# An attention block with two feed-forward layers: sums of the first block products drawn ahead, and the last stores of the first layer moved to ScalarE's queue

## The chip, the cores and the metric

The kernel runs on one core of a Trainium2 chip, in one launch. The metric is the device time in microseconds (us). Five engines have instruction streams of their own: TensorE (PE; its weight loads are shown as PEld), VectorE (DVE), ScalarE (ACT), GpSimd (POOL) and SyncE (SP). SP does no arithmetic here; it issues DMA transfers, one after the other in its program's order, and a transfer whose condition is not met holds up all that stand behind it. ScalarE can issue transfers as well, in the order of its own stream. An instruction on any engine starts when the semaphores that it waits for have been raised by the instructions or transfers that it depends on.

## The reference, cut to what matters

```python
# q, k, v: 4 batches x 8 heads x 768 positions x 64;  mem_k, mem_v: 8 positions more
for c in range(768 // 32):                  # chunks of 32 queries
    k_ctx, v_ctx = positions 32c-16 .. 32c+40, cut at the ends
    scores = (q_c @ concat(mem_k, k_ctx).T) / 8
    a = exp(scores - max); a = a / (sum(a) + 1e-9)
    out_c = a @ concat(mem_v, v_ctx)
x = out as 3072 tokens x 512
h = x @ w_in                                # 512 x 2048
x = maximum(0.01 * h, h) @ w_out            # 2048 x 512
out = ((x @ w_a) * (x @ w_b)) @ w2_out      # 512 x 1536, 512 x 1536, 1536 x 512
```

All values are float32.

## The kernel before, in words

**Precision.** TensorE is fed with a rounded part and a remainder of each operand: ScalarE casts a tile to the rounded type ("hi", names like `xh`, `gh`, `ch`), VectorE subtracts it from the original ("lo", `xl`, `gl`, `cl`), and each product is three matmuls: hi·hi, hi·lo, lo·hi.

**Blocks and items.** The 3072 tokens are six blocks of 512, counted from 0. For blocks 0 to 3 the first layer runs as a list of items (block, f), where f is one of 16 slices of 128 hidden units. An item has 12 matmuls `h<-xh,w`, `h<-xl,w` (lines 435 to 437), a leaky relu on ScalarE (`g<-h`, L527), its cast (`gh<-g`, L530) and remainder (`gl<-g,gh`, L533), and two items later 12 matmuls of `mm2` (L559 to 563) that add to four PSUM banks `a`. At the last f of a block, `mm2` copies each of the four banks with ScalarE to a tile `x2` (written `x` in the trace, tag `z`, three buffers), and SP stores it to the block's DRAM array `x2d` (L576, L577). In this text item i means the i-th of the items of blocks 0 to 3 (i = 16 · block + f), so the last is item 63.

**Attention beside the items.** The 24 attention units (128 tokens each) run between the items. `STARTS` says at which item unit k of the last sixteen begins: scores and the first half of the softmax at item i, the rest of the softmax at i+1, sixteen 32-wide transposes on VectorE (`pt<-p`, L348) at i+2, and at i+3 the product with the values on TensorE (`pv<-pt,v`, L388) and a copy of it into the token tiles (`a_out`; `a_raw` for blocks 4 and 5, into `xr`). A unit of block 4 that is done before `xr` exists (item 48) is stored to DRAM (`x4d`) and read back. The preparation of the second layer's weights is spread over the same items.

**Block products.** Blocks 4 and 5 of the first layer go together through seven products of half-size blocks instead of eight. Token sums `y` come from `xr` (VectorE subtractions in `y_sub`, ScalarE cast and VectorE remainder in `y_part`), weight sums from `w` (`s_sums`: two additions `zs`, tag `z`, and four `sc`; `s_parts`: cast and remainder `sw`). `prod` runs six matmuls into a bank `A`, `B` or `C`; a loop over p takes the 16 slices in eight pairs. In it, `snapped` copies a bank to a tile `u` with ScalarE, `summed` adds a bank to it on VectorE (`s`), and the sum goes through the leaky relu (`g<-s`) and `mm2`. TensorE, VectorE and ScalarE keep the written order here (class `InOrder`; its helper lines L46 and L49 stand for the line in many rows). SP's order comes from a scheduler.

**What comes behind.** Block 5 ends with 16 calls of `mm2` on kept values, with w_out tiles read back on SP (`wo_load`, L853). Its last call again makes four copies and four stores. The second layer follows: `wab_load` (L1094) fetches weights (`wab<-wab`, 512 KB each, five buffers in a pool that takes the place of the first layer's weight pool), and its first matmuls are `ca<-ch,wab`, six to a bank. `xs_load` (L803) reads blocks of `x2d` back for it.

Of the kernel before, what the change touches and what calls it, by code (L numbers as in the profile page):

```python
# [55 lines left out]
def kernel(  # L56
# [355 lines left out]
    def x_raw():  # L412
        for h, tag in enumerate(("xh", "xl")):
            xr[NL + h] = xp.tile([P, KC, TB], F32, tag=tag, name="xr")
        for k in x4d:
            sp.dma_start(out=xr[NL][:, :, k * UT:k * UT + UT], in_=x4d[k])
# [10 lines left out]
    def x_tiles(key):  # L427
        hi = xp.tile([P, KC, TB], F32R, tag="xh", name="xh")
        lo = xp.tile([P, KC, TB], F32R, tag="xl", name="xl")
        x1[key] = (hi, lo)  # L430
# [109 lines left out]
    def mm1(bi, parts):  # L540
        return mm1_act(*mm1_pe(bi, parts))

    def mm2(bi, parts, g):
        if bi not in acc:
            last = bi == NB3 - 1
            acc[bi] = [
                p.tile([P, TB], F32, tag=t, name="a")
                for p, t in (((ps_h, "h"), (ps_s, "s")) * 2 if last else ((ps_a, "a"),) * KC)
            ]
        gh, gl = g  # L550
        for o, n, f in parts:
            slot = wslot[f, 1]
            t = slice(o, o + n)
            for e in range(KC):
                ps = acc[bi][e][:, t]
                c = slice(e * P, e * P + P)

                kw = dict(skip_group_check=bi == 0)
                pe.matmul(  # L559
                    ps, slot[:, 1, c], gh[:, t], start=f == 0 and o == 0, stop=False, **kw  # L560
                )
                pe.matmul(ps, slot[:, 0, c], gl[:, t], start=False, stop=False, **kw)  # L562
                pe.matmul(  # L563
                    ps, slot[:, 0, c], gh[:, t], start=False,
                    stop=f == NF1 - 1 or (o == HALF and f == LEAD - 1), **kw
                )
            if bi == 0:
                ready = {(0, NF1 - 1): slice(0, HALF), (HALF, LEAD - 1): slice(HALF, TB)}
                t = ready.get((o, f))
            else:  # L570
                t = t if f == NF1 - 1 else None
            if t is not None:
                for e in range(KC):
                    ps = acc[bi][e][:, t]
                    y = tp.tile([P, TB], F32, tag="z", name="x2", bufs=3)
                    act.copy(y[:, t], ps)  # L576
                    sp.dma_start(out=x2d[bi][:, e, t], in_=y[:, t])  # L577

    HALF, LEAD = TB // 2, 3
    items = []  # L580
# [94 lines left out]
    def at_item(i, *args):  # L675
        at(*divmod(i, NF1), *args)

    STARTS = (17, 20, 23, 26, 29, 32, 34, 37, 40, 42, 45, 48, 50, 53, 56, 59)
    for k, i in enumerate(STARTS):
        u = 2 * TB // UT + k  # L680
        blk, o = divmod(SEQ[u], TB // UT)
# [19 lines left out]
    def prep_load(upto):  # L701
        while len(raws) < min(upto, len(sources)):
            raw = prep.tile([P, 512, 2], I32, tag="raw", name="raw", bufs=4)
            nc.sync.dma_start(
                out=raw.rearrange("p n w -> p (n w)"),
                in_=w2_l[sources[len(raws)]].bitcast(I32),
            )
            raws.append(raw)
# [138 lines left out]
    def wo_load(upto):  # L847
        while wo_next[0] < upto:
            b, f = 1 + wo_next[0] // NF1, wo_next[0] % NF1
            if b == NB3:  # L850
                break
            t = wop.tile([P, 2, 512], F32R, tag="wo", name="w")
            nc.sync.dma_start(out=t.bitcast(F32), in_=wod[f])  # L853
            wslot[f, 1] = t
            wo_next[0] += 1

    x_tiles(("x", 1))
    behind += first_items()
    STEPS = 58
    for bi, f, parts in items[LEAD:]:  # L860
        first = bi == 0
        if f == 0 and not first:
            if bi + 1 < NL:
                x_tiles(("x", bi + 1))
            else:
                x_raw()
        if first:
            W1.load(2 * f + 14)
            W1.step()
        behind.append((bi, parts, mm1(bi, parts)))  # L870
        if first:
            W1.step()
        if len(behind) > LAG:
            mm2(*behind.pop(0))
        for fn in beside.get((bi, f), []):
            fn()
        if not first:
            wo_load((bi - 1) * NF1 + f + 4)

            i = (bi - 1) * NF1 + f  # L880
            n = (NL - 1) * NF1
            for _ in range(STEPS * (i + 1) // n - STEPS * i // n):
                next(steps, None)
        elif f >= NF1 - 1:
            wo_load(f - NF1 + 2)
            prep_load(f - NF1 + 1)


    att.__exit__(None, None, None)
    xa_pool = tc.tile_pool(name="xa", bufs=1, side="left", reuse_waits="tile")  # L890
    xa = xa_pool.__enter__()
    ya, hc, homes = {}, KC // 2, {}
    two = "p k n -> p (k n)"

# [11 lines left out]
        return homes[key][:, h]  # L906

    def y_part(i):
        t = Y[i].rearrange(two)
        hi, lo = [y_home(i, l) for l in range(2)]  # L910
        ya[i] = hi, lo
        hi, lo = hi.rearrange(two), lo.rearrange(two)
        act.copy(hi, t)
        dve.tensor_tensor(out=lo, in0=t, in1=hi.bitcast(F32), op=ALU.subtract)

    b11, b21, b12, b22 = [
        xr[NL + h][:, k * hc:k * hc + hc] for h in range(2) for k in range(2)
    ]
    Y = (b11, b21, b21, b12, b12, b11, b22)

    def y_sub(out, x, y):
        dve.tensor_tensor(out=out, in0=x, in1=y, op=ALU.subtract)

    sums_, sw = {}, {}

# [18 lines left out]
    def s_parts(p, h):  # L944
        t = sums_[p][h]
        w = xa.tile([P, 2, 2, 256], F32R, tag="sw", name="sw", bufs=3)
        act.copy(w[:, 0], t)
        dve.tensor_tensor(out=w[:, 1], in0=t, in1=w[:, 0].bitcast(F32), op=ALU.subtract)
        for k, n in enumerate(((2, 3), (4, 6))[h]):
            sw[p, n] = w[:, :, k]  # L950

    def prod(ps, p, n, i, first):
# [6 lines left out]
        for kc in range(hc):  # L959
# [3 lines left out]
            pe.matmul(ps, w[:, 0, c], lo[:, kc], start=False, stop=False, **kw)  # L963
            pe.matmul(ps, w[:, 0, c], hi[:, kc], start=False, stop=kc == hc - 1, **kw)

    def relu(src, kept=None):
        g = tp.tile([P, TB], F32, tag="t", name="g")
        act.activation(g, src, AF.Prelu, alpha=0.01)
        if kept is None:
            gh = tp.tile([P, TB], F32R, tag="gh", name="gh", bufs=3)  # L970
            gl = tp.tile([P, TB], F32R, tag="gl", name="gl", bufs=3)
        else:
            w = wp.tile([P, 2, TB], F32R, tag=f"wi{kept}", name="g5")
            gh, gl = w[:, 0], w[:, 1]
        act.copy(gh, g)

        def low():
            dve.tensor_tensor(out=gl, in0=g, in1=gh.bitcast(F32), op=ALU.subtract)
            return gh, gl

        return low

    def snapped(ps):
        t = tp.tile([P, TB], F32, tag="t", name="u")
        act.copy(t, ps)
        return t
# [17 lines left out]
    def part2(bi, f, g):  # L1004
        return bi, [(0, TB, f)], g

    y_part(0)
    y_part(1)
    next2(behind.pop(0))
    y_sub(b12, b12, b11)  # L1010
    y_part(3)
    y_sub(b12, b22, b12)
    s_sums(0)
    s_parts(0, 0)
    y_part(4)
    y_sub(b11, b12, b11)
    y_part(5)
    s_parts(0, 1)
    y_sub(b21, b21, b12)
    y_part(2)  # L1020
    y_part(6)

    kept, late = {}, None
    for p in range(NF1 // 2):
        f0, f1 = 2 * p, 2 * p + 1
        A = ps_h.tile([P, TB], F32, tag="h", name="A")
        prod(A, p, 0, 0, True)
        Bk = ps_s.tile([P, TB], F32, tag="s", name="B")
        if p:
            act.copy(Bk, A)  # L1030
            low12 = relu(late, f1 - 2)
        else:
            a1 = snapped(A)
        next2(behind.pop(0))
        if p:
            kept[f0 - 2] = low12()
        prod(Bk, p, 1, 1, p == 0)
        if p:
            next(steps, None)
        if p + 1 < NF1 // 2:  # L1040
            s_sums(p + 1)
        low11 = relu(Bk if p else summed(a1, Bk))
        g11 = low11()
        prod(A, p, 2, 4, False)
        u2 = snapped(A)
        C = ps_s.tile([P, TB], F32, tag="s", name="C")
        prod(C, p, 3, 3, True)
        if p + 1 < NF1 // 2:
            s_parts(p + 1, 0)
            s_parts(p + 1, 1)  # L1050
        prod(A, p, 4, 5, False)
        u3 = snapped(A)
        s22 = summed(u3, C)
        next2(part2(NL, f0, g11))
        kept[f1] = relu(s22, f0)()
        if p:
            next(steps, None)
        prod(A, p, 5, 2, False)
        low21 = relu(A)
        prod(C, p, 6, 6, False)  # L1060
        behind.append(part2(NL, f1, low21()))
        late = summed(u2, C)
# [519 lines left out]
```

## Time and profile before

| | |
|---|---|
| time, median of 3 runs | 1146.26 us (1146.11 to 1147.21) |
| the profiled execution's own time | 1146.38 us |
| its span in the profile | 1144.6 us |
| TensorE busy | 1105.0 us (97%) |
| VectorE busy | 776.0 us (68%) |
| ScalarE busy | 527.3 us (46%) |
| mean granted TensorE clock | 0.987 |
| DMA moved | 270.63 MB, mean 236 GB/s |

The profile is of one execution. A row of the timeline gives the start, the duration, the engine, the line, the operation with out<-in and, in square brackets, how long the engine was idle before it and what ended that idle time. A row "x3" sums up three instructions in a run. In window rows "PEclk" is the mean granted TensorE clock as a share of full speed: 1.00 is 2.4 GHz, 0.50 is 1.2 GHz. The time of the profiled execution is 1.78 us longer than its span.

### The profile page before, as it was taken

What the parts mean: (1) busy time and instruction counts of PE and PEld (TensorE: products, weight loads), DVE (VectorE), ACT (ScalarE), POOL (GpSimd) and SP (SyncE); (2) the same over time, 40 slices, a digit from 0 to 9 for tenths busy, and PEclk for the clock granted to TensorE, in tenths of its full rate; (3) what the DMA queues carried; (4) which work ended last, traced back from release to release, by engine and by line L of the source; (5) the groups of instructions that cost most, each with busy time, mean ns of one, the idle gap of its engine ahead of it and who ended that gap; (6) DMA issues with size and microseconds to landing.
All of it is one profiled execution on the core that took longest, in us unless ns stands there. A gap on an engine that the chain in (4) does not pass through costs nothing.

```text
span 1144.6 us, 16319 instructions
## 1 busy us (share of the span) xinstructions
PE 1105.0 (97%) x6194; PEld 912.8 (80%) x6194; DVE 776.0 (68%) x1418; ACT 527.3 (46%) x893; POOL 6.3 (1%) x16
## 2 busy tenths in 40 slices
PE   7899999999999995999997999999999999999997
PEld 6788888888888883888886888888888888888886
DVE  6897389888988765666540555668755668755666
ACT  5886555556555434565521343233343233343232
POOL 2000000000000000000000000000000000000000
PEclk9999999999999997999998999999999999999999
DMA  9996799999999912443485947476877476757452
GB/s 322 396 354 234 247 350 328 338 314 337 322 321 338 332 70 92 157 157 133 164 338 173 309 135 252 134 251 188 242 240 251 136 249 188 235 176 248 139 194 74
DMA packets 99854, 270.63 MB, mean 236 GB/s; under 512 B 9664, under 2 KB 24128, under 8 KB 99008
## 3 DMA queue, kind: packets, MB, share of 16 engines
q1 hardware_dynamic: 98608, 268.93, 69.7%
q8 instruction: 49, 0.80, 0.3%
q10 hardware_dynamic: 1168, 0.66, 0.2%
q14 instruction: 29, 0.24, 0.1%
HBM read 215.02 MB, written 54.53 MB: 235 GB/s over the span
## 4 chain that ended last, share of the span: by engine, by line
PE 92%; DVE 2%; ACT 2%; DMA 2%; issue 1%; SPq 0%; DVEq 0%; ACTq 0%
PE ca L49 18%; PE cc L49 9%; PE oa L49 8%; PE a L49 8%; PE h L435 5%; PE a L559 5%; PE h L436 5%; PE h L437 5%; PE a L562 5%; PE a L563 5%; PE cb L49 5%; PE oy L49 4%; PE A L49 4%; PE pv L388 2%; PE s L279 2%; PE C L49 2%
## 5 line engine op out<-in xcount | busy, mean ns | idle before, releaser
L49 PE MATMUL ca<-ch,wab 128*128 128x512 f32 x576 | 193.1, 391 | 6.3 <-DMA wab<-wab 6.3
L49 ACT CAST st<-gb 128x512 fp32r<-128x512 f32 x126 | 76.5, 621 | 124.4 <-DVE gb L49 121.0
L49 PEld LDWEIGHTS ca<-ch,wab 128*128 128x128 f32 x576 | 108.6, 189 | 29.7 <-issue 6.7
L49 PE MATMUL ca<-cl,wab 128*128 128x512 f32 x288 | 112.6, 391 | 0.0
L49 PE MATMUL oa<-st,wt 128*128 128x512 f32 x420 | 104.3, 389 | 0.0
L435 PE MATMUL h<-xh,w 128*128 128x512 f32 (+1 forms) x256 | 101.7, 397 | 0.7 <-ACT xh L49 0.7
L49 PE MATMUL cc<-ch,wab 128*128 128x512 f32 x288 | 100.3, 389 | 0.0
L436 PE MATMUL h<-xl,w 128*128 128x512 f32 (+1 forms) x256 | 98.7, 386 | 0.2 <-DVE xl L49 0.2
L437 PE MATMUL h<-xh,w 128*128 128x512 f32 (+1 forms) x256 | 98.7, 385 | 0.0
L559 PE MATMUL a<-gh,w 128*128 128x512 f32 (+1 forms) x256 | 97.7, 382 | 0.3 <-ACT x L576 0.3
L562 PE MATMUL a<-gl,w 128*128 128x512 f32 (+1 forms) x256 | 97.5, 381 | 0.0
L563 PE MATMUL a<-gh,w 128*128 128x512 f32 (+1 forms) x256 | 97.4, 381 | 0.0
L49 DVE TENSOR_TENSOR st<-gb,st 128x512 fp32r<-128x512 f32 x126 | 85.3, 689 | 15.0 <-ACT st L49 13.2
L49 PEld LDWEIGHTS oa<-st,wt 128*128 128x128 f32 x420 | 78.8, 188 | 16.4
L49 ACT COPY u<-ca 128x512 f32<-128x512 f32 x72 | 42.3, 587 | 92.4 <-PE ca L49 92.3
L348 DVE STREAM_TRANSPOSE pt<-p 32x128 f32<-32x128 f32 x256 | 77.4, 302 | 4.3
L49 PEld LDWEIGHTS ca<-cl,wab 128*128 128x128 f32 x288 | 54.3, 189 | 11.1
L49 PEld LDWEIGHTS cc<-ch,wab 128*128 128x128 f32 x288 | 54.1, 188 | 11.3
L533 DVE TENSOR_TENSOR gl<-g,gh 128x512 fp32r<-128x512 f32 (+1 forms) x64 | 43.2, 675 | 22.2 <-ACT gh L530 18.5
L435 PEld LDWEIGHTS h<-xh,w 128*128 128x128 f32 x256 | 48.1, 188 | 11.3 <-ACT xh L49 0.8
L559 PEld LDWEIGHTS a<-gh,w 128*128 128x128 f32 x256 | 48.1, 188 | 10.1 <-ACT x L576 0.8
L49 PE MATMUL cc<-cl,wab 128*128 128x512 f32 x144 | 56.0, 389 | 0.0
(189 smaller groups left out, 2043.3 us busy)
## 6 DMA issues: line engine op xcount, KB each, us to landing
wab<-wab SPq DMA_DIRECT2D x126, 512.0 KB, 4.4
w<-wod SPq DMA_DIRECT2D x80, 512.0 KB, 5.4
raw<-w SPq DMA_DIRECT2D x68, 512.0 KB, 6.9
wt<-wtd SPq DMA_DIRECT2D x63, 512.0 KB, 4.7
k<-kl SPq DMA_DIRECT2D x48, 256.0 KB, 5.3
v<-vl SPq DMA_DIRECT2D x48, 256.0 KB, 5.1
wab<-pwb SPq DMA_DIRECT2D x12, 768.0 KB, 6.9
wod<-w SPq DMA_DIRECT2D x16, 512.0 KB, 6.6
```

What stands on the lines that cost most here:

```text
L49: self.last = emit(*args, **kwargs).ins
L279: pe.matmul(s[64 * cpar:64 * cpar + 64, cp * 4 + hp, :], qb[:, o, :], k[:, r:r + 64], start=True, stop=True,)
L348: dve.transpose(out=pt[o0:o0 + 32, :, 2 * cpar + hpar, hpx, :], in_=p[i0:i0 + 32, hpx::2, 32 * b:32 * b + 32],)
L388: pe.matmul(o[64 * hpar:64 * hpar + 64, 2 * pair:2 * pair + 2, t0:t0 + CH], v[:, i:i + 64], pt[:, 2 * cp + pair, 2 * cpar + hpar].rearrang ...
L435: pe.matmul(ps, w[1], x[0], start=first, stop=False)
L436: pe.matmul(ps, w[0], x[1], start=False, stop=False)
L437: pe.matmul(ps, w[0], x[0], start=False, stop=last)
L533: dve.tensor_tensor(out=gl[:, c], in0=g[:, c], in1=gh[:, c].bitcast(F32), op=ALU.subtract)
L559: pe.matmul(ps, slot[:, 1, c], gh[:, t], start=f == 0 and o == 0, stop=False, **kw)
L562: pe.matmul(ps, slot[:, 0, c], gl[:, t], start=False, stop=False, **kw)
L563: pe.matmul(ps, slot[:, 0, c], gh[:, t], start=False, stop=f == NF1 - 1 or (o == HALF and f == LEAD - 1), **kw)
```

## The change

Three things change, and no matmul is added or taken away. The last block's four stores are issued by ScalarE instead of SP. The last eight attention units begin zero, one or two items earlier: 40, 42, 45, 48, 50, 53, 56, 59 become 39, 42, 44, 47, 49, 52, 54, 57. And part of the token and weight sums of the first block products is attached to items 60, 61 and 62 instead of standing behind item 63; what is left is spread over the first pass of the loop over p.

```diff
-                    sp.dma_start(out=x2d[bi][:, e, t], in_=y[:, t])
+                    (act if bi == NB3 - 1 else sp).dma_start(out=x2d[bi][:, e, t], in_=y[:, t])
...
-    STARTS = (17, 20, 23, 26, 29, 32, 34, 37, 40, 42, 45, 48, 50, 53, 56, 59)
+    STARTS = (17, 20, 23, 26, 29, 32, 34, 37, 39, 42, 44, 47, 49, 52, 54, 57)
...
+    def y_begin():
+        nonlocal xa
+        att.__exit__(None, None, None)
+        xa = xa_pool.__enter__()
+        y_part(0)
+        y_part(1)
...
+    def y_subs():
+        y_sub(2, 2, 0)
+        y_part(3)
+        y_sub(2, 3, 2)
+        y_sub(0, 2, 0)
+        y_sub(1, 1, 2)
+
+    def s_begin():
+        s_sums(0)
+        s_parts(0, 0)
+        s_parts(0, 1)
...
+    at_item(max(STARTS) + 3, y_begin)
+    at_item(max(STARTS) + 4, y_subs)
+    at_item(max(STARTS) + 5, s_begin)
...
-    y_part(0)
-    y_part(1)
     next2(behind.pop(0))
-    y_sub(b12, b12, b11)
-    y_part(3)
-    y_sub(b12, b22, b12)
-    s_sums(0)
-    s_parts(0, 0)
     y_part(4)
-    y_sub(b11, b12, b11)
     y_part(5)
-    s_parts(0, 1)
-    y_sub(b21, b21, b12)
-    y_part(2)
-    y_part(6)
...
         else:
             a1 = snapped(A)
+            y_part(2)
         next2(behind.pop(0))
...
         u2 = snapped(A)
+        if p == 0:
+            y_part(6)
         C = ps_s.tile([P, TB], F32, tag="s", name="C")
```

`y_part`, `y_sub`, `s_sums`, `s_parts` and `prod` themselves do what they did; they stand ahead of the item loop now.

ScalarE's stream at the first block products, before, from the end of the last attention unit to the copies of block 3's result. `y` are the token sums' casts, `sw` the weight sums' casts, `u<-A` is the copy `a1` of the first product's bank, `x` the copies of the result:

```order
L46 CAST y<-xr 128x1024
L49 CAST y<-xr 128x1024
L527 ACTIVATE g<-h 128x512
L530 CAST gh<-g 128x512
L49 CAST y<-xr 128x1024
L49 CAST sw<-sc 128x512
L49 CAST y<-xr 128x1024 x2
L49 CAST sw<-sc 128x512
L49 CAST y<-xr 128x1024 x2
L49 COPY u<-A 128x512
L49 COPY x_4898<-a 128x512
```

The same stretch after, from the leaky relu of the last item to the second bank copy `u<-A`, called `u2` in the code:

```order
L527 ACTIVATE g<-h 128x512
L46 CAST y<-xr 128x1024
L530 CAST gh<-g 128x512
L49 CAST y<-xr 128x1024
L49 COPY u<-A 128x512
L49 CAST y<-xr 128x1024
L49 COPY x_4899<-a 128x512
L49 COPY x_4902<-a 128x512
L49 COPY x_4905<-a 128x512
L49 COPY x_4908<-a 128x512
L49 ACTIVATE g<-s 128x512
L49 CAST gh<-g 128x512
```

Before, seven `y` casts and two `sw` casts stand ahead of the first `u<-A`. After, three `y` casts and both `sw` casts stand ahead of this piece, two `y` casts stand in it ahead of `u<-A`, one behind `u<-A`, and the last one behind the second `u<-A`, which follows `gh<-g`.

SP's stream at the end of the first layer, before: the last three w_out tiles, the stores of block 5's result (`x2d_91`), and the second layer's first weights.

```order
L853 DMA w<-wod_105 128x1024
L853 DMA w<-wod_106 128x1024
L853 DMA w<-wod_107 128x1024
L577 DMA x2d_91<-x_6223 128x512
L577 DMA x2d_91<-x_6226 128x512
L577 DMA x2d_91<-x_6229 128x512
L1094 DMA wab<-wab_111 128x1024
L577 DMA x2d_91<-x_6232 128x512
L1094 DMA wab<-wab_111 128x1024 x5
```

SP's stream at the same place, after (the line of `wab_load` is 1106 there):

```order
L853 DMA w<-wod_105 128x1024
L853 DMA w<-wod_106 128x1024
L853 DMA w<-wod_107 128x1024
L1106 DMA wab<-wab_111 128x1024 x7
L1123 DMA wt<-wtd_108 128x1024 x2
```

The weight loads follow the last w_out tile directly. The stores stand in ScalarE's stream, each behind the copy that feeds it and ahead of the next copy.

## Rows read from the trace of the kernel before

**Rows 1.** Waits of TensorE: engine, line, releaser: us in total, times, longest.

```profile
PE A L49 <- ACT u L49: 14.1, 2, 9.1
PE ca L49 <- DMA wab<-wab: 6.3, 1, 6.3
```

**Rows 2.** Timeline of the first stall, 423 to 442 us.

```profile
423.77 1.05 ACT L49 CAST y<-xr 128x1024 fp32r<-128x1024 f32 x1 [0.91 <-DVE xr L49]
...
426.84 1.52 PE L49 MATMUL A<-y,w 128*128 128x512 f32 x6
...
430.92 1.52 PE L49 MATMUL B<-y,w 128*128 128x512 f32 x6
...
440.90 0.58 ACT L49 COPY u<-A 128x512 f32<-128x512 f32 x1
...
441.53 2.93 PE L49 MATMUL A<-y,sw 128*128 128x512 f32 x6 [9.08 <-ACT u L49]
```

**Rows 3.** Timeline of the second stall, 441 to 452 us.

```profile
441.99 1.31 SPq L577 DMA_DIRECT2D x2d<-x  x3
443.36 0.45 SPq L803 DMA_DIRECT2D xs<-x2d  x1
...
444.25 2.67 PE L49 MATMUL C<-y,sw 128*128 128x512 f32 x6
444.57 0.59 ACT L49 COPY x<-a 128x512 f32<-128x512 f32 x1 [1.63 <-DMA x2d<-x]
...
446.65 1.29 DVE L49 TENSOR_TENSOR zs<-w 128x512 f32<-128x512 f32 x2 [4.40 <-DMA x2d<-x]
...
449.46 0.68 DVE L49 TENSOR_TENSOR s<-u,B 128x512 f32<-128x512 f32 x1
...
451.36 0.58 ACT L49 COPY u<-A 128x512 f32<-128x512 f32 x1
...
451.99 2.93 PE L49 MATMUL A<-y,sw 128*128 128x512 f32 x6 [5.06 <-ACT u L49]
```

**Rows 4.** Windows: stretch, length, busy us, then PEclk, DMA share, GB/s.

```profile
441.50:446.90 5.40, 5.37 (x12) 3.80 (x12) 1.00 (x2) 2.02 (x4) 0.00 (x0) 0.52 0.83 215
...
452.00:457.00 5.00, 5.00 (x12) 3.94 (x13) 2.16 (x4) 2.24 (x5) 0.00 (x0) 0.51 0.01 3
...
620.50:624.30 3.80, 3.79 (x9) 3.03 (x10) 0.00 (x0) 0.59 (x1) 0.00 (x0) 0.51 1.00 405
...
320.00:380.00 60.00, 60.00 (x427) 49.43 (x426) 51.24 (x126) 33.44 (x53) 0.00 (x0) 1.00 0.95 337
...
410.00:420.00 10.00, 10.00 (x72) 8.15 (x71) 2.31 (x6) 3.19 (x6) 0.00 (x0) 1.00 0.29 97
```

**Rows 5.** Timeline of the third stall, 593 to 621 us.

```profile
593.68 4.52 SPq L853 DMA_DIRECT2D w<-wod  x3
...
612.83 1.68 SPq L577 DMA_DIRECT2D x2d<-x  x3
614.56 0.46 SPq L1094 DMA_DIRECT2D wab<-wab  x1
615.40 0.59 ACT L49 COPY x<-a 128x512 f32<-128x512 f32 x1 [1.24 <-DMA x2d<-x]
...
620.51 0.77 PE L49 MATMUL ca<-ch,wab 128*128 128x512 f32 x1 [6.34 <-DMA wab<-wab]
```

**Rows 6.** The stores at L577: us from issue to landing, 28 transfers.

```profile
DMA to landing us min/median/max: 1.9/3.1/7.3
```

**Rows 7.** The page, part 6: weight loads of the second layer, KB, us to landing.

```profile
wab<-wab SPq DMA_DIRECT2D x126, 512.0 KB, 4.4
```

**Rows 8.** Line L1302: issues on ScalarE's queue, ns min/median/max.

```profile
L1302 ACTq DMA_DIRECT2D out<-y x4: 382/907/1326, 1137.8 to 1140.2; - x4
```

**Rows 9.** Timeline of an attention unit: last transposes, then the product with the values.

```profile
305.69 3.82 DVE L348 STREAM_TRANSPOSE pt<-p 32x128 f32<-32x128 f32 x12
...
311.18 1.15 PE L388 MATMUL pv<-pt,v 128*64 128x64 f32 x32
```

More of the change, by code (lines that the diff above doesn't have):

```diff
@@ L858 @@
     behind += first_items()
[L859 to L889, printed above, removed]
     xa_pool = tc.tile_pool(name="xa", bufs=1, side="left", reuse_waits="tile")
-    xa = xa_pool.__enter__()
+    xa = None
     ya, hc, homes = {}, KC // 2, {}
@@ L908, in y_part @@
     def y_part(i):
-        t = Y[i].rearrange(two)
+        t = y_raw(Y[i]).rearrange(two)
         hi, lo = [y_home(i, l) for l in range(2)]
@@ L914, in y_part, with y_raw, y_sub @@
         dve.tensor_tensor(out=lo, in0=t, in1=hi.bitcast(F32), op=ALU.subtract)
[L916 to L922, printed above, removed]
+    def y_raw(c):
+        return xr[NL + c // 2][:, c % 2 * hc:c % 2 * hc + hc]
+    Y = (0, 1, 1, 2, 2, 0, 3)
+    def y_sub(o, x, y):
+        dve.tensor_tensor(out=y_raw(o), in0=y_raw(x), in1=y_raw(y), op=ALU.subtract)
+    def y_begin():
[14 more added lines that the diff above has]
+        s_parts(0, 1)
     sums_, sw = {}, {}
@@ L964, in prod @@
             pe.matmul(ps, w[:, 0, c], hi[:, kc], start=False, stop=kc == hc - 1, **kw)
+    at_item(max(STARTS) + 3, y_begin)
+    at_item(max(STARTS) + 4, y_subs)
+    at_item(max(STARTS) + 5, s_begin)
+    STEPS = 58
+    for bi, f, parts in items[LEAD:]:
+        first = bi == 0
+        if f == 0 and not first:
+            if bi + 1 < NL:
+                x_tiles(("x", bi + 1))
+            else:
+                x_raw()
+        if first:
+            W1.load(2 * f + 14)
+            W1.step()
+        behind.append((bi, parts, mm1(bi, parts)))
+        if first:
+            W1.step()
+        if len(behind) > LAG:
+            mm2(*behind.pop(0))
+        for fn in beside.get((bi, f), []):
+            fn()
+        if not first:
+            wo_load((bi - 1) * NF1 + f + 4)
+            i = (bi - 1) * NF1 + f
+            n = (NL - 1) * NF1
+            for _ in range(STEPS * (i + 1) // n - STEPS * i // n):
+                next(steps, None)
+        elif f >= NF1 - 1:
+            wo_load(f - NF1 + 2)
+            prep_load(f - NF1 + 1)
     def relu(src, kept=None):
```

## The prediction

> **What bounds the kernel now.** The first view is the list of TensorE's waits [rows 1]. Two entries hold most of what it loses: 14.1 us in two waits for a `u` copy by ScalarE, the longest of 9.1, and one wait of 6.3 us for the second layer's first weights. The change touches these three stalls, so the timeline is read around each.
>
> First stall [rows 2]: TensorE begins `B` at 430.92. From `A` at 426.84 to there it issues 18 matmuls in 4.08 us, 0.227 us each, so six take 1.36 and `B` is through at about 432.3. The next `A` starts only at 441.53, after 9.08 idle us, released by `u<-A` at 440.90. That copy is 0.58 us of work, and the bank it reads was complete at 426.84 + 1.36 = 428.2. It was late because it stands in ScalarE's order behind all the `y` and `sw` casts (1.05 us for a `y` cast), each of which waits for a VectorE subtraction.
>
> Second stall [rows 3]: `A` and `C` run until 446.9, then TensorE waits 5.06 us for the second `u<-A`, at 451.36. That stands behind `g<-s`, which waits for `s<-u,B` at 449.46; `s` stands in VectorE's order behind `zs` at 446.65, which waited 4.40 us for stores of block 3's result to free the `z` buffers. From `zs` to TensorE's restart is 451.99 - 446.65 = 5.34 us.
>
> Third stall [rows 5]: the matmul `ca` starts at 620.51 after 6.34 us, so TensorE had stopped at 614.17. SP issued the first weight load at 614.56, right behind three stores (612.83, 1.68 us) that need the block's last matmuls, while its transfer before those, the last of three w_out loads, was issued by 593.68 + 4.52 = 598.2. For 14.6 us SP's queue stood behind a store that could not start.
>
> The windows add what a stall costs beyond itself [rows 4]. Behind each one the granted clock is 0.51 or 0.52, the level of 1.2 GHz: 12 matmuls take 5.37 us behind the first, 5.00 behind the second, 9 take 3.79 behind the third. At 0.227 each they would take 2.72, 2.72 and 2.04, so the clock costs 2.65, 2.28 and 1.75 us.
>
> **The token and weight sums.** No matmul and no cast is added. Ahead of the first `u<-A`, ScalarE now has, from the last item's relu on, one relu, one `gh` cast and two `y` casts, under 4 us from about 421.6, so the copy is ready to run at 428.2; I take 428.4 to 429.0. The 9.08 us go, and with them the slow clock behind them: `B` ends at 432.3, `A` at 433.6, `C` at 435.0.
>
> What is late next is the second `u<-A`. Its chain is unchanged: it stands behind `g<-s`, that behind `zs`, that behind the stores that hold the `z` buffers. The copies `x` are now at 430.0, 430.5 and 431.0 (one `y` cast comes between `u` and them), the second store is issued near 431.0 (stores issue 1.31 / 3 = 0.44 us apart [rows 3]). Before, the first store landed 444.57 - 441.99 = 2.6 us after its issue, and the second, issued near 442.4, released `zs` at 446.65, 4.2 us after it; there a 1 MB load (L803) was issued at 443.36, 0.9 us behind it, and in the changed order it stands behind a VectorE remainder that comes after the stall. The median store lands in 3.1 us [rows 6]. I take 3.1, since nothing shares the DMA engines then: `zs` at 434.2, restart at 439.6. By 4.2 it is 440.6. TensorE's restart moves from 451.99 to 439.6, 12.4 us earlier (11.4 by 4.2). A stall of 439.6 - 435.0 = 4.6 us stays. Whether the clock falls in it no row shows: the shortest stall that I have is 5.06 us, and there it was low already. I take the low clock, so that the 2.28 us behind this stall stay in the sum.
>
> The moved VectorE work (token parts, subtractions, `zs`, `sc`) costs nothing: it goes to items 60 to 62, beside a stretch like 410 to 420, where VectorE is busy 2.31 of 10 us [rows 4]. A `gl` that has to stand behind a subtraction is late by about 1.2 us, and its matmuls come two items of 24 × 0.227 = 5.4 us later. If that cover failed, TensorE would lose at most the excess over it, under 1 us.
>
> **The attention units.** Seven of the last eight units begin one or two items earlier; their spacing alternates between two and three items. It can bring nothing by itself, since TensorE is busy 60.00 of 60 us from 320 to 380 [rows 4]. It can cost, because the sixteen transposes of a unit must be done when TensorE reaches `pv`: at the tightest place that I found they end at 305.69 + 3.82 = 309.51 and `pv` starts at 311.18, a slack of 1.67 us [rows 9]. VectorE is busy 51.24 of 60 us there [rows 4], 0.85; 18 items instead of 19 for the same units raise that by a factor of 19/18 to 0.90 at most. That stretch already holds two units two items apart (48 and 50) without a stall. If nothing of the added density were absorbed, it would be the excess of 0.85 / 18 = 0.047 over 18 items of 5.44 us, 4.6 us; that is the upper end, nothing the lower. I take 0.2, near the row without stalls. One more unit of block 4 is done before `xr` exists, so a 256 KB store and its reload are added on SP; the reload is needed from item 60 on, twelve items later.
>
> **The last stores.** SP now issues the weight loads directly behind the w_out loads, and the ones that the first products need wait for no store. With 4.4 us to landing [rows 7] against 16 us to spare, the first `ca` finds its weights: 6.34 us and the 1.75 us of slow clock go, 8.1 together. Four tiles, each for two products of six matmuls, cover 4 × 2.72 = 10.9 us, to 625.0; the fifth load waits for the first store's landing, near 615.4 [rows 5], and lands at 619.8.
>
> What is added stands in ScalarE's order: four issues between the copies, ahead of the first copy `a<-ca`, for which the third bank of six matmuls waits at 614.17 + 2.72 = 616.9. The trace has no such store there. The nearest row is the output's stores from ScalarE: 0.38, 0.91 and 1.33 us (smallest, median, largest of four) [rows 8]. With 0.38 the fourth copy still waits for the first store, at 615.4, its issue ends at 616.4, and `a<-ca` at 617.0: 0.1 us late. With 0.91 it is 612.83 + 4 × 0.91 + 3 × 0.59 + 0.58 = 618.8, 1.9 late; with 1.33 it is 620.5, 3.6 late. I take 0.38, because SP's issues of the same stores, 1.68 / 3 = 0.56 each, are nearer to it than to the median. This part then brings 8.0 us, between 4.5 and 8.1.
>
> The Trainium skill speaks against this part ("DMA: Bandwidth & Descriptors", section "Issuing engines are not separate DMA queues"): transfers that ScalarE or SyncE starts run on the same 16 DMA engines and interleave, so that a second issuer saves only sequencer issue time. By that rule alone the gain would be the 1.68 us of SP's three issues and not 8.0. Here the trace differs in what stood in the way: the loads' issue waited 14.6 us for a condition of the stores, not for DMA engines.
>
> **Sum.** 1146.38 (the profiled execution: span 1144.6 and 1.78 around it) - 12.4 - 8.0 + 0.2 = 1126.2 us. The profiled execution is 0.12 above the median of the runs, less than any term is known to; I leave the sum as it is.
>
> **Rivals.**
> Clock kept: the shorter second stall leaves the clock at full speed, and another 2.28 us go: 1123.9. For it: 4.6 us is below every stall that I could read. Against it: the stalls of 5.06 and 6.34 us both end with the low clock.
>
> Late stores or late transposes: stores take up to 7.3 us [rows 6]. With that landing `zs` is at 438.3 and the restart at 443.6: 4.0 us less gain, 1130.2. The upper end of the attention cost gives 1130.6. For it: the row's maximum and VectorE's density; against: the DMA engines are hardly used around 410 to 420 (share 0.29 [rows 4]).
>
> Loads that come no earlier: if the weight loads are held to the end of the block by their buffers, only 1.68 us of the third stall go: 1146.38 - 12.4 - 1.7 + 0.2 = 1132.5. For it: buffers of the second layer take the place of the first layer's. Against it: SP's stream had just the stores between w_out and these loads. This is also where the skill's rule ends.
>
> Slower: transposes on VectorE become the bound of the attention items. To end over 1146.38 by the 0.2% (2.3 us) that a measurement of this kernel can tell from no change, the seven moved units must cost 20.4 + 2.3 = 22.7 us, 3.2 each, so their transposes must come 1.67 + 3.2 = 4.9 us later than in the tightest place now, almost a whole item. VectorE at 0.90 speaks against it; it would decide only from about 1.0. The time would be 1148.7 or more.
>
> **Chances.** Forecast 0.62 (1125 to 1128), clock kept 0.18, late stores or transposes 0.11, loads no earlier 0.05, slower 0.02, gains that cancel to within 0.2% 0.02. The likeliest is 1126.2. The range of 1122.8 to 1131.0 holds the first three cases and most of ScalarE's issue price. Faster 0.96, same 0.02, slower 0.02.
>
> **What the changed profile would show.** TensorE's first wait for `u` is gone, and `B`, `A`, `C` follow each other from the last `mm2` on. One wait of 4 to 6 us for `u` remains, with `zs` behind a store of `x2d`, and the granted clock around it decides between the forecast and the first rival. No wait for `wab` at the start of the second layer; the loads lie near 600. If the `u` wait is over 7 us, the landing was mis-sized; if `pv` waits for transposes by more than a few us in all, the units are too dense; if `ca` waits for `a<-ca`, ScalarE's issues are dearer than 0.38 us. A time above 1131 makes the forecast wrong.

## The result, and the profile after

| | before | after |
|---|---|---|
| median of 4 runs | 1146.74 us (1146.11 to 1149.06) | 1127.95 us (1126.89 to 1128.85) |
| span of the profiled execution | 1144.6 us | 1125.4 us |
| mean granted TensorE clock | 0.987 | 0.995 |

The ratio is 0.9832, with a 95% interval of 0.9814 to 0.985: about 19 us less, where 20.2 were forecast. 1127.95 lies in the range given. The profiled execution took 1127.18 us, 1.78 around its span as before, so the spans may be subtracted: 19.2 us.

TensorE's list of waits in the changed kernel, in the columns of [rows 1], holds these two among its first five entries:

```profile
PE A L49 <- ACT u L49: 4.1, 1, 4.1
...
PE a L559 <- ACT x L576: 0.7, 1, 0.7
```

One `u` wait is left of two, the `wab` wait is gone, and a wait for a copy `x` at L576 is larger than it was. The timeline of the changed kernel around the first two stalls shows where the time came from:

```profile
428.59 1.52 PE L49 MATMUL A<-y,w 128*128 128x512 f32 x6
...
430.15 0.59 ACT L49 COPY u<-A 128x512 f32<-128x512 f32 x1 [3.80 <-PE A L49]
...
432.20 1.31 SPq L577 DMA_DIRECT2D x2d<-x  x3
...
432.67 1.52 PE L49 MATMUL B<-y,w 128*128 128x512 f32 x6
...
434.03 1.52 PE L49 MATMUL A<-y,sw 128*128 128x512 f32 x6
...
435.39 1.52 PE L49 MATMUL C<-y,sw 128*128 128x512 f32 x6
435.62 1.34 DVE L49 TENSOR_TENSOR zs<-w 128x512 f32<-128x512 f32 x2 [2.67 <-DMA x2d<-x]
...
438.46 0.68 DVE L49 TENSOR_TENSOR s<-u,B 128x512 f32<-128x512 f32 x1
...
440.36 0.58 ACT L49 COPY u<-A 128x512 f32<-128x512 f32 x1
...
440.99 2.93 PE L49 MATMUL A<-y,sw 128*128 128x512 f32 x6 [4.08 <-ACT u L49]
```

The first `u<-A` waits only for `A` itself, and `B`, `A`, `C` follow each other 1.36 us apart. Against [rows 2, 3] TensorE's restart moved from 451.99 to 440.99, 11.0 us. The wait that stays is the chain of [rows 3]: store, `zs`, `s`, `g`, `u`. The windows (length, busy time of PE, PEld, DVE, ACT and POOL with the number of instructions, then clock, DMA share, GB/s as in [rows 4]) show that the clock did fall in it:

```profile
436.70:441.10 4.40, 0.32 (x2) 0.11 (x1) 2.99 (x7) 1.89 (x4) 0.00 (x0) 0.81 0.20 78
441.10:446.00 4.90, 4.90 (x12) 3.83 (x13) 3.20 (x5) 3.08 (x6) 0.00 (x0) 0.50 0.38 110
```

Behind the stall 12 matmuls take 4.90 us at 0.50, the level of 1.2 GHz, as before. At the end of the first layer:

```profile
587.35 22.11 SPq L1106 DMA_DIRECT2D wab<-wab  x7
...
601.93 0.36 ACTq L49 DMA_DIRECT2D x2d<-x  x1
...
603.11 0.39 PE L49 MATMUL ca<-ch,wab 128*128 128x512 f32 x1
...
605.46 0.59 ACT L49 COPY a<-ca 128x512 f32<-128x512 f32 x1 [0.40 <-ACT x L49]
```

The weight loads begin at 587.35, in the place where SP's queue stood still in [rows 5], and `ca` starts with no wait at full clock. `ca` moved from 620.51 to 603.11, 17.40 us; 11.0 of them are from before, so 6.4 are the stall, and the remaining 19.2 - 17.4 = 1.8 lie behind it, the slow clock.

### The profile page after: what moved, and what is told of

It reads as the page before. It is cut to its first block, busy times and chain, and to the rows that moved or that the text cites. A ratio compares the mean times of both kernels' runs of the same rounds, so it can differ in the third digit from the quotient of the medians.

```text
span 1125.4 us, 16314 instructions
## 1 busy us (share of the span) xinstructions
PE 1102.2 (98%) x6194; PEld 911.5 (81%) x6194; DVE 773.9 (69%) x1418; ACT 526.8 (47%) x893; POOL 6.3 (1%) x16
## 4 chain that ended last, share of the span: by engine, by line
PE 91%; ACT 3%; issue 2%; DVE 2%; DMA 1%; ACTq 0%; SPq 0%; DVEq 0%
PE ca L49 18%; PE cc L49 9%; PE oa L49 8%; PE a L49 6%; PE h L435 5%; PE h L436 5%; PE h L437 5%; PE a L559 5%; PE a L562 5%; PE a L563 5%; PE cb L49 5%; PE oy L49 4%; PE A L49 4%; PE pv L388 2%; PE s L279 2%
## 5 line engine op out<-in xcount | busy, mean ns | idle before, releaser
L436 PE MATMUL h<-xl,w 128*128 128x512 f32 (+1 forms) x256 | 98.7, 386 | 0.2 <-DVE xl L49 0.2
L559 PE MATMUL a<-gh,w 128*128 128x512 f32 (+1 forms) x256 | 97.7, 382 | 0.7 <-ACT x L576 0.7
L562 PE MATMUL a<-gl,w 128*128 128x512 f32 (+1 forms) x256 | 97.5, 381 | 0.0
L563 PE MATMUL a<-gh,w 128*128 128x512 f32 (+1 forms) x256 | 97.4, 381 | 0.0
L559 PEld LDWEIGHTS a<-gh,w 128*128 128x128 f32 x256 | 48.1, 188 | 10.5 <-ACT x L576 1.2
L527 ACT ACTIVATE g<-h 128x512 f32<-128x512 f32 (+1 forms) x64 | 37.2, 581 | 41.0 <-PE h L437 40.7
```

The lines of the kernel that those rows point to most:

```text
L436: pe.matmul(ps, w[0], x[1], start=False, stop=False)
L527: act.activation(g[:, c], ps[:, c], AF.Prelu, alpha=0.01)
L559: pe.matmul(ps, slot[:, 1, c], gh[:, t], start=f == 0 and o == 0, stop=False, **kw)
L563: pe.matmul(ps, slot[:, 0, c], gh[:, t], start=False, stop=f == NF1 - 1 or (o == HALF and f == LEAD - 1), **kw)
```

## The experiments

Each ratio is against the kernel before, measured beside the run (median 1146.7 to 1147.1 us), with its 95% interval. Gains in us against the kernel before are worked out from the ratio.

**Each part alone.** The first edit is the stores alone.

```diff
 # kernel before
-                    sp.dma_start(out=x2d[bi][:, e, t], in_=y[:, t])
+                    (act if bi == NB3 - 1 else sp).dma_start(out=x2d[bi][:, e, t], in_=y[:, t])
```

> The kernel before with one edit: ScalarE issues the last block's four stores. Theory (the two parts of the change are independent; the weight loads stood behind stores in SP's order): the 6.3 us wait of the first ca matmul and the slow clock behind it go, 8.2 us less, 1138.5 against 1146.7; the two u waits of 9.1 and 5.1 us stay. Rival (a second issuing engine saves issue time alone): 1.7 us less, 1145.0, and the wait for wab is still 4 to 6 us.

Measured 1138.78 us, ratio 0.9930 (0.9918 to 0.9943), 8.0 us less. The wait for `wab` is gone and both `u` waits stay (14.4 us together). The second takes the changed kernel and gives the stores back to SP.

```diff
 # changed kernel
-                    (act if bi == NB3 - 1 else sp).dma_start(out=x2d[bi][:, e, t], in_=y[:, t])
+                    sp.dma_start(out=x2d[bi][:, e, t], in_=y[:, t])
```

> The changed kernel with the last stores back on SP: sums ahead and earlier units alone. Theory: 11.0 us less than before, 1135.7; one u wait of about 4.1 us, the wait for wab of about 6.3 us back, with the slow clock behind it. Rival (the parts interact): more than 13 us or less than 9 us less.

Measured 1135.47 us, 0.9903 (0.9889 to 0.9917), 11.1 us less. Its waits are 5.6 us for `wab` and 4.1 for one `u`.

8.0 + 11.1 = 19.1: the parts add up, and each is worth what its stall showed.

**Is it the issuing engine or the order?** The stores go back to SP, but the first four weight loads are put ahead of them (`issue_after` sets an instruction behind another in its engine's order; the weight pool and its loader move up with the loads).

```diff
 # changed kernel; loads emitted four slices before the end of block 5
-                    (act if bi == NB3 - 1 else sp).dma_start(out=x2d[bi][:, e, t], in_=y[:, t])
+                    if bi == NB3 - 1:
+                        with tc.issue_after(wab_last[0]):
+                            sp.dma_start(out=x2d[bi][:, e, t], in_=y[:, t])
+                    else:
+                        sp.dma_start(out=x2d[bi][:, e, t], in_=y[:, t])
...
     for f in range(NF1):
+        if f == NF1 - 4:
+            wab_load(4)
         next2(part2(NL + 1, f, kept[f]))
```

> The changed kernel with the last block's stores back on SP, but the second layer's first four weight loads put ahead of them in SP's order. Theory (the stall came from the order on one queue, not from which engine issues): ca waits for no wab, as in the changed kernel, 1127 to 1129. Rival (a second issuer is needed): ca waits 3 us or more for a load or for ScalarE's copies, 1131 or more.

Measured 1128.03 us, 0.9838 (0.9824 to 0.9851), the same as the changed kernel's 0.9832. SP's queue and the first product:

```profile
587.55 1.85 SPq L1102 DMA_DIRECT2D wab<-wab  x4
602.12 1.68 SPq L579 DMA_DIRECT2D x2d<-x  x3
...
603.30 0.39 PE L49 MATMUL ca<-ch,wab 128*128 128x512 f32 x1
```

The four loads are at 587.55, the stores at 602.12 on the same queue, and `ca` waits for no `wab`. What counted is that none of the first four loads stood behind a store that had to wait; the second issuer was one way to that.

**Units or sums?** The kernel before gets the new start items alone.

```diff
 # kernel before
-    STARTS = (..., 37, 40, 42, 45, 48, 50, 53, 56, 59)
+    STARTS = (..., 37, 39, 42, 44, 47, 49, 52, 54, 57)
```

> The kernel before with the eight new start items alone; the sums stay behind the item loop. Theory (the 1.75 us by which the changed kernel reaches the last mm2 later come from the units' places): the first block products start 1.5 to 1.8 us later than before, at 428.3 to 428.6 instead of 426.84, no stall gets shorter, 1148.2 to 1148.5. Rival (the loss comes from the sums beside the items): the same time as before, 1146.7, with A at 426.8.

Both theories failed: 1140.63 us, 0.9949 (0.9937 to 0.9962), 5.8 us less. The timeline of this kernel:

```profile
430.49 1.52 PE L49 MATMUL A<-y,w 128*128 128x512 f32 x6
...
438.46 1.67 PE L49 MATMUL A<-y,sw 128*128 128x512 f32 x6 [2.37 <-ACT u L49]
...
448.26 2.93 PE L49 MATMUL A<-y,sw 128*128 128x512 f32 x6 [6.74 <-ACT u L49]
```

`A` does start later, 430.49, where the first theory had 428.3 to 428.6; 1.60 us of that lie ahead of the first moved unit, where a `pv` starts at 174.43 instead of 172.83. But with the last unit done two items sooner the first sums begin by themselves beside the last items, although they are written behind them (the items' own order comes from the scheduler), and the first stall shrinks from 9.08 to 2.37 us. The second grows from 5.06 to 6.74 us, so the two together fall from 14.1 to 9.1. The opposite test keeps the old start items and moves only the sums.

```diff
 # changed kernel
-    STARTS = (..., 37, 39, 42, 44, 47, 49, 52, 54, 57)
+    STARTS = (..., 37, 40, 42, 45, 48, 50, 53, 56, 59)
...
-    at_item(max(STARTS) + 5, s_begin)
+    at_item(max(STARTS) + 4, s_begin)
```

> The changed kernel with the old start items; the sums then begin at items 62 and 63 (both of the last steps at 63). Theory (the units had to move so that VectorE's 12 us of sums fit ahead of the last item): TensorE reaches A at 426.8, waits about 4 us for u at 432.3 to 436.2, then again about 5 us, restart near 446.5; 1133.0. Rival (the sums fit without moving the units, and the units' cost is saved): 1126.2 or less, first u wait gone.

The rival held in its mechanism, though not with its 1126.2: 1127.50 us, 0.9832 (0.9818 to 0.9845), the changed kernel's ratio; the forecast of 1133.0 was wrong. I had put the `sw` casts ahead of `u<-A`; they stand behind it:

```profile
429.67 0.59 ACT L49 COPY u<-A 128x512 f32<-128x512 f32 x1 [0.19 <-PE A L49]
...
430.15 1.14 ACT L935 CAST sw<-sc 128x512 fp32r<-128x512 f32 x2
...
442.08 2.93 PE L49 MATMUL A<-y,sw 128*128 128x512 f32 x6 [5.66 <-ACT u L49]
...
447.62 1.52 PE L49 MATMUL A<-y,w 128*128 128x512 f32 x6
```

The first `u` wait is gone without moving a unit. `A` starts 0.5 us sooner than in the changed kernel, at 428.11 (1.7 sooner, if one counts from a `pv` ahead of the first moved unit, as below), but the second wait is 5.66 us, so TensorE restarts 1.09 us later, at 442.08. The changed kernel has lost that lead 18 matmuls on:

```profile
447.64 1.52 PE L49 MATMUL A<-y,w 128*128 128x512 f32 x6
```

From the restart to there these 18 take 5.54 us here and 6.65 in the changed kernel, where at 0.227 each they would take 4.08. So in this execution the slow clock behind the stall cost 1.46 us instead of 2.57, and that is why the two profiled executions end within 0.2 us of each other. Moving the units and moving the sums are two ways to the first stall. The second removes it whole, the first most of it.

**What the moved units cost.** From one `pv` at about 172.8 us, ahead of the first moved unit, to the first `A` the five kernels with the old starts (before, the stores alone, the sums with old starts, and two reordered ones below) need 254.01 to 254.40 us. Six with the new starts need 255.60 to 256.74 (the seventh, the doubled stores below, has a slow clock in this stretch and needs 258.85). In each of the six TensorE waits 0.5 to 1.7 us for the fourth `x` copy of block 2 (L576); with that wait taken off, all six are within 255.04 to 255.10, or 1.05 us longer than the kernel before. TensorE behind this wait in the changed kernel:

```profile
344.64 0.50 PE L559 MATMUL a<-gh,w 128*128 128x512 f32 x1 [0.73 <-ACT x L576]
```

For the 1.05 us, compare TensorE around a `pv` that stands alone (changed kernel) with a `pv` with scores `s` behind it (kernel before):

```profile
312.14 0.39 PE L563 MATMUL a<-gh,w 128*128 128x512 f32 x1
...
312.46 1.15 PE L388 MATMUL pv<-pt,v 128*64 128x64 f32 x32
313.55 0.50 PE L435 MATMUL h<-xh,w 128*128 128x512 f32 x1
...
313.88 0.39 PE L436 MATMUL h<-xl,w 128*128 128x512 f32 x1
```

```profile
329.42 0.39 PE L563 MATMUL a<-gh,w 128*128 128x512 f32 x1
...
329.74 1.15 PE L388 MATMUL pv<-pt,v 128*64 128x64 f32 x32
330.72 1.10 PE L279 MATMUL s<-k,qz 128*64 128x64 f32 x32
331.75 0.50 PE L435 MATMUL h<-xh,w 128*128 128x512 f32 x1
332.09 0.39 PE L436 MATMUL h<-xl,w 128*128 128x512 f32 x1
```

From L563 to L436 the lone one takes 1.74 us, the pair 2.67. Less the two ordinary steps of 0.227 that each stretch holds, that is 1.29 and 2.22. Scores that stand alone cost 1.29 as well, so a pair saves 0.36; all the pairs and lone groups from 292 to 420 us in both kernels give these numbers to 0.01. The tile column changes between 128\*128 and 128\*64 there. The Trainium skill ("TensorEngine Tiling (Array Packing)", section "Key Properties") says that a change of tiling mode drains the engine; the rows agree, with 0.36 us for the two changes that a pair saves, though they do not show the draining itself. A pair occurs where two starts lie three items apart: seven times from item 34 on before, five after. To test it, one start was moved in the kernel before, which takes away two pairs and leaves the end in place.

```diff
 # kernel before
-    STARTS = (..., 40, 42, 45, 48, 50, 53, 56, 59)
+    STARTS = (..., 40, 42, 46, 48, 50, 53, 56, 59)
```

> The kernel before with one start item moved, 45 to 46: two units fewer begin in an item in which another unit's pv stands, and the last unit ends where it did. Theory (TensorE loses about 0.38 us for each pair of pv and scores that no longer stand side by side): from the pv at 172.8 to the first A of the block products it takes 254.8 instead of 254.0 us. Rival (the places of pv and scores cost nothing, the 1.05 us come from the units being denser): 254.0.

One run: 1147.5 us. From `pv` at 172.04 to `A` at 428.98 it takes 256.94 us, 2.93 more. 1.6 are two waits for `x` copies, 1.3 remain. That is more than the 0.76 expected: the rival's 254.0 is excluded, but 0.7 of it is the pairs by the rows, and each wait also costs a refill (L562 follows 0.33 us behind the waiting L559 at 344.64, 0.10 more than the pitch). Some 0.2 to 0.4 us stay unexplained, here and in the 1.05.

**What holds the wait that is left.** Block 3's stores were doubled.

```diff
 # changed kernel
+                    if bi == NL - 1:
+                        again = dp.tile([P, TB], F32, tag=f"again{e}", name=f"again{e}")
+                        sp.dma_start(out=again, in_=y[:, t])
```

> The changed kernel, with each of block 3's four stores followed by a second store of the same tile to a DRAM array that nobody reads. Theory (the u wait that is left hangs on the landing of these stores through the z buffers): zs starts 1.5 to 2.5 us later behind the stores, and TensorE's wait for u grows from 4.1 by as much, to 5.6 to 6.6 us. Rival (another wait ends last there): the wait for u stays at 4.1 us.

One run: 1130.92 us. The wait for `u` is 5.55 us:

```profile
438.33 1.52 PE L49 MATMUL C<-y,sw 128*128 128x512 f32 x6
...
440.68 0.69 DVE L49 TENSOR_TENSOR zs<-w 128x512 f32<-128x512 f32 x1 [0.52 <-DMA again<-x]
...
445.40 2.93 PE L49 MATMUL A<-y,sw 128*128 128x512 f32 x6 [5.55 <-ACT u L49]
```

The second `zs` begins 2.35 us behind `C`, in the changed kernel 435.62 + 1.34 - 0.69 - 435.39 = 0.88: it is 1.47 us later, and the wait is 1.47 longer, just under the low end of what was expected. So the stores' landing is what releases the chain. The rest of the time lies elsewhere: the wait for block 2's `x` copy is 2.34 us in this execution, and the window behind it shows the slow clock:

```profile
346.10:349.50 3.40, 3.38 (x36) 2.53 (x36) 3.32 (x9) 1.08 (x2) 0.00 (x0) 0.52 0.71 193
```

The second way to test it is to shorten the chain: `s` and its remainder stand ahead of the next pair's sums.

```diff
 # changed kernel
-        if p + 1 < NF1 // 2:
+        if p and p + 1 < NF1 // 2:
             s_sums(p + 1)
         low11 = relu(Bk if p else summed(a1, Bk))
         g11 = low11()
+        if p == 0:
+            s_sums(1)
```

> The changed kernel; in the first pass VectorE adds s and the remainder gl ahead of the next pair's weight sums zs and sc, instead of behind them. Theory (the u wait that is left, 4.1 us, is the chain store, zs, sc, s, g, u): s starts when the second store lands, near 435.6, TensorE restarts near 438.3, the stall is 1.5 us and the clock stays at 1.00: 4.8 us less than the changed kernel, 1123.2. Rival (ScalarE's copies and the stores' landing set it, whatever stands between): same time, 1127.9.

Measured 1124.37 us, 0.9802 (0.9789 to 0.9816); against 1128.0 that is 3.6 less. Timeline and window:

```profile
437.03 0.69 DVE L49 TENSOR_TENSOR s<-u,B 128x512 f32<-128x512 f32 x1 [2.72 <-PE A L49]
...
439.57 1.66 PE L49 MATMUL A<-y,sw 128*128 128x512 f32 x6 [1.29 <-ACT u L49]
```

```profile
436.00:442.00 6.00, 4.71 (x22) 3.56 (x21) 3.55 (x7) 3.09 (x6) 0.00 (x0) 1.00 0.44 157
```

The stall is 1.29 us and the clock stays at 1.00, as expected. The first row names a matmul into `A`, which `s` does not read; the second store, issued near 433.56 + 0.44, would by 2.98 us have landed at 436.98, so it is the likelier releaser. Of the 4.8 us forecast the profiled execution has 3.1 when it comes to `ca` (600.01 against 603.11): it reached `A` at 429.96, 1.4 later than the profiled one of the changed kernel, and it was as late already at the `pv` ahead of the first moved unit, 174.36 against 172.81. Next, `u2` is copied ahead of `g<-s` as well.

```diff
 # changed kernel; takes the place of the last edit
-        if p + 1 < NF1 // 2:
+        if p and p + 1 < NF1 // 2:
             s_sums(p + 1)
-        low11 = relu(Bk if p else summed(a1, Bk))
-        g11 = low11()
+        s11 = Bk if p else summed(a1, Bk)
+        if p:
+            g11 = relu(s11)()
         prod(A, p, 2, 4, False)
         u2 = snapped(A)
         if p == 0:
+            g11 = relu(s11)()
+            s_sums(1)
             y_part(6)
```

> As the kernel with s ahead of zs, and in the first pass ScalarE copies u2 ahead of g<-s. Theory: A's bank is free at 436, TensorE goes on after C without a wait for u, at most 0.5 us for gh or gl, clock 1.00: 6.3 us less than the changed kernel, 1121.6. Rival (the wait turns into one of the mm2 for gh or gl of 2 us or more): 1123.5 to 1125.5.

Measured 1124.23 us, 0.9802 (0.9789 to 0.9816): nothing over the last one, so the 1121.6 was wrong. The 1.3 us wait is gone, but not for one of 2 us for `gh` or `gl`, as the rival had it: the copy `u3` stands behind casts that wait for `sc`, and TensorE now waits 1.15 us there.

The same two edits with the old start items and the sums at items 62 and 63:

> The kernel with both reorderings and the old start items, sums beginning at items 62 and 63. Theory (the sums' places bring the gain, the units' places nothing): within 1 us of the kernel with both reorderings, 1121 to 1122.6. Rival (the two or three items more that the sums have matter once the second wait is gone): a new wait for y or sw parts of 2 us or more, 1124 or more.

1123.48 us, 0.9798 (0.9785 to 0.9811), the same within the intervals. Its waits are 0.9 and 0.2 us for `gh` and `gl` and 1.2 for `u`, and `A` starts at 428.13. The last kernel removes those.

```diff
 # on top of it, in the first pass
+            s11 = tp.tile([P, TB], F32, tag="t", name="s")
+            dve.tensor_tensor(out=s11, in0=a1, in1=Bk, op=ALU.add)
...
-        if p + 1 < NF1 // 2:
+        if p and p + 1 < NF1 // 2:
             s_parts(p + 1, 0)
             s_parts(p + 1, 1)
         prod(A, p, 4, 5, False)
         u3 = snapped(A)
         s22 = summed(u3, C)
+        if p == 0:
+            s_parts(1, 0)
+            s_parts(1, 1)
```

> The kernel with both reorderings and the old start items, and two more edits in the first pass: s goes to a tile of another tag, so that it waits for no store, and the casts sw of the next pair stand behind the copy u3 in ScalarE's order. Theory (what was left are the 0.9 and 0.2 us waits for gh and gl and the 1.2 us wait for u behind those casts, 2.3 us): all three go, 1121.2. Rival (the next wait in the pass comes up at once, for s22 or the sw parts): 1122.5 to 1123.5.

1120.56 us, 0.9776 (0.9762 to 0.9789): 26 us under the kernel before, and 6.4 us by the ratios, 7.4 by the medians, under the changed one. TensorE goes on behind `C` with no wait for `u`, and 0.37 us for `s` is the longest wait left in the first pass. With its other tag `s` starts at 434.00, with no wait for a store:

```profile
433.86 1.52 PE L49 MATMUL C<-y,sw 128*128 128x512 f32 x6
434.00 0.68 DVE L49 TENSOR_TENSOR s<-u,B 128x512 f32<-128x512 f32 x1
...
441.85 1.65 PE L49 MATMUL C<-y,sw 128*128 128x512 f32 x6 [0.37 <-DVE s L49]
```

## Why the prediction was right, point by point

- **The first stall** went as said, with the clock behind it. The first `u<-A` waits for its bank alone. Only the reading of what held it was too broad: of the nine casts ahead of it in the kernel before, four started with no idle time on ScalarE, and the longest wait, 4.67 us, was that of a `sw` cast for `sc`.
- **What comes next in its place** was named rightly: the second `u`, by the chain from the stores. The landing was taken as 3.1 us; the second store, issued near 432.20 + 0.44, freed `zs` at 435.62, 2.98 us later. The wait was put at 4.6 and is 4.08 us, and the clock fell in it, as chosen. The doubled stores and the shortened chain show the mechanism.
- **The last stores** were put at 8.0 us and measured 8.0 alone and 8.2 in the spans. ScalarE's issues cost 0.33 to 0.36 us, just under the smallest of [rows 8], so `a<-ca` is hardly late: the third bank of `ca` starts 0.27 us behind the pitch. By the Trainium skill's rule on issuing engines, as the prediction cites it, the gain would have been 1.7 us; the kernel with both on SP, loads first, shows why it does not decide here.
- **The moved units** are the term that was mis-sized: 0.2 us taken, 1.77 measured in the profiled execution (255.78 against 254.01 us from the `pv` to `A`, of which 0.73 is one wait), up to 2.7 in the others of the six. The upper end of 4.6 held, but its mechanism, VectorE's density and late transposes, is not what cost: in the changed kernel's list of TensorE's waits from 172 to 433 us no `pv` stands. TensorE waited for a copy on ScalarE, and lost pairs of `pv` and scores. The sentence that moving the units "can bring nothing by itself" was wrong as well: without the moved sums it brings 5.8 us, because the first sums behind the units move with them.
- **The sum**: 12.4 + 8.0 - 0.2 was forecast. The spans give 11.0 + 8.2. 12.4, 0.5 more from the shorter wait and 1.8 less for the units make 11.1. That the sum came within 1.0 us is in part luck: the units' term was off by 1.6, and the two smaller errors, 0.5 and 0.2, went the other way.

Of the rivals, late stores, loads that come no earlier and the clock kept did not occur, and the slower side's mechanism did not show.

## What to carry to other kernels

A transfer that must wait for a computation holds up everything behind it on its queue: look in the issuing engine's stream for what stands behind it, and either put that ahead or give the waiting transfer another issuer; here both ended at the same time. When a stall is removed, follow the chain of the next one to its first releaser at once: reordering one pass of the loop, with the units left where they were, brought 6 to 7 us more. Two edits made together may be two ways to the same gain; run each alone before crediting both.

## What the runs showed of the hardware

Stalls of 1.29 and 1.70 us (the latter for block 2's `x` copy, with the stores back on SP) left the clock at 1.00. One of 2.34 us (the doubled stores) and one of 4.08 had 0.50 to 0.52 behind them, while one of 2.37 us (the new starts alone, `A` in 1.67 us behind it) did not: two stalls of almost the same length ended differently. Nor did the longer stall cost more slow clock: behind one of 4.08 us it cost 2.57 us, behind one of 5.66 us (the sums with old starts) 1.46. A group of 32 small matmuls at tile 128\*64 between 128\*128 ones costs 1.29 us alone and 2.22 as a pair with another such group. Issuing a 256 KB store on ScalarE took 0.33 to 0.36 us at the end of the first layer, where [rows 8] has 0.38 to 1.33.
